# Two transfers over 128 partitions cut into pieces of 32 partitions, in a fused attention and two-layer MLP kernel

## The chip, the cores and the metric

The kernel runs on one core of one Trainium2 chip. The metric is the device time in microseconds (us), the median of several executions. One further execution was taken with the hardware profiler, and its trace is what the prediction reads.

## The reference

Three stages are fused. The input arrays q, k and v have the shape (1, 6016, 256).

```
qn = q / (norm(q, axis=1) + 1e-6);  kn = k / (norm(k, axis=1) + 1e-6)
s = kn.T @ qn / tau                     # 256 x 256, summed over the 6016 rows
a = softmax(s, axis=-1)
x = v @ a                               # 6016 x 256
x = elu(x @ moe_w_in) @ moe_w_out       # 256 -> 2048 -> 256
x = silu(x @ moe2_w_in) @ moe2_w_out    # 256 -> 2048 -> 256
```

## The kernel before

The 6016 rows are 47 blocks of 128, in six groups of eight blocks (the last has seven). The program has three parts.

**Start.** The arrays q and k stream through a buffer named `ring`; TensorE sums the scores, ScalarE and VectorE the squares of the columns (`sums`). Towards its end the first group of v is loaded into the tile `v0` by two transfers (line 461), each of 512 KB: 128 partitions by 4 blocks of 256 numbers. The row `i*32 + b*8 + j` of the group goes to partition `32*b + i`, and the view of v on the DRAM side therefore has `b` (4) outermost and `i` (32) inside it. After the softmax TensorE transposes `v0` (line 491).

**Main part.** From line 520 on the operations are recorded, put in an order by `in_order` with costs that the kernel states, and then emitted. All recorded operations go through a few helpers, so that one line stands for many of them: line 229 is every matrix product, line 200 every ScalarE operation, line 206 every VectorE operation on two tensors, and line 218 every transfer. Layer 1 runs over the six groups, then layer 2. Weights come through the buffers `st`, are converted (`cv`), and end in `wa`, `a21` and `wo`; the later groups of v come through `big`, eight transfers of 32 partitions for a group, in runs of 128 bytes. The tile `wa` lies in the memory of `v0`, so its first writers wait for the transfers into `v0` too.

**End.** The last group is stored by `y_store_final`, once for each half (`half` is 1, then 0): VectorE copies one PSUM bank (line 799) and ScalarE another into a `big` buffer, and one transfer of 512 KB stores it. The DRAM side of it is `rows_of[:, :, ...]`, with `b` outermost again.

Every transfer is issued by SyncE (SP), in the program's order. Eight completion semaphores, which the rows of the program's order name DMAHW0 to DMAHW7, are used in rotation: a transfer takes the next one, and SP first waits until the transfer eight before it, which used the same one, has landed.

Of the kernel before, what the change touches and what calls it, by code (L numbers as in the profile page):

```python
# [19 lines left out]
P = 128  # L20
# [19 lines left out]
V = namedtuple("V", "ap keys")  # L40
# [67 lines left out]
def channel_attention_elu_silu(  # L108
# [28 lines left out]
    nc = tc.nc  # L137
# [6 lines left out]
    TJ = 4  # L144
# [9 lines left out]
    vv = v.rearrange("b n c -> (b n) c")  # L154
# [9 lines left out]
    v0 = one.tile([P, GJ, C], F32, tag="wa", name="v0")  # L164
# [12 lines left out]
    def do(engine, n, emit, reads, writes, times=1):  # L177
        fixed, each, late, own = COST[engine]
        o = Op(
            engine,  # L180
            times * (fixed + each * n),
            late,
            own,
            emit,
            [k for v in reads if isinstance(v, V) for k in v.keys],
            [k for v in writes for k in v.keys],
        )
        if recording:
            ops.append(o)
        else:  # L190
            emit()
# [10 lines left out]
    def copy(out, src, **kw):  # L202
        act(out, src, AF.Copy, **kw)
# [13 lines left out]
    def dma(out, src):  # L217
        do("SP", 0, lambda: nc.sync.dma_start(out.ap, src.ap), [src], [out])  # L218
# [28 lines left out]
    def part(v, ap, *what):  # L247
        return V(ap, tuple(v.keys[0]._replace(what=x) for x in what))
# [15 lines left out]
    def y_bank(i):  # L264
        return V(y_ps[i], (("y", i),))
# [99 lines left out]
    with tc.manual_schedule():  # L365
# [92 lines left out]
        j0, nj0 = groups[0]  # L458
        for n in range(2):
            s = slice(n * nj0 // 2, (n + 1) * nj0 // 2)  # L460
            nc.sync.dma_start(v0[:, s], vv[: nj0 * P].rearrange("(i b j) c -> b i j c", i=32, b=4)[:, :, s])
        x, nr, r, t1, hx = nsq[:, 0:4], small[:, 4:8], small[:, 8:12], small[:, 12:16], small[:, 28:32]
        nc.scalar.activation(nr, x, AF.Sqrt)
        nc.scalar.activation(small[:, 25:26], one_sb, AF.Exp)
# [328 lines left out]
        def y_store_final(half):  # L793
            j0, nj = groups[order[final][1]]
            o = bigs.take()
            n = TJ * C
            y = [y_bank(2 * half + i) for i in range(2)]
            o0, o1 = (part(o, o.ap[:, i * n // 2 : (i + 1) * n // 2], i) for i in range(2))
            do("DVE", n // 2, lambda: nc.vector.tensor_copy(o0.ap, y[0].ap), [y[0]], [o0])
            copy(o1, y[1])  # L800
            rows_of = out[j0 * P : (j0 + nj) * P].rearrange("(i b j) c -> b i j c", i=32, b=4)
            dma(
                V(rows_of[:, :, half * TJ : (half + 1) * TJ], ()),
                part(o, o.ap[:, :n].rearrange("p (j c) -> p j c", j=TJ), 0, 1),
            )


        m_group(0)
# [4 lines left out]
        for s in range(len(steps) + 1):  # L813
            prev = s - 1
            now = s < len(steps)
            if now:
                n, j = steps[s]
# [17 lines left out]
            if s:  # L835
                second(prev, (0, 1))
                if steps[prev] == (final, NP - 1):
                    y_store_final(1)
                second(prev, (0, 0))
                if steps[prev][1] == NP - 1:  # L840
                    if steps[prev][0] == final:
                        y_store_final(0)
                    else:
                        y_store(steps[prev][0])
# [36 lines left out]
```

## Time and profile before

| what | value |
| --- | --- |
| median of 3 executions | 1088.67 us (1086.88 to 1089.07) |
| the profiled execution | 1089.08 us |
| its span, first to last instruction | 1087.3 us |
| TensorE busy | 1051.7 us, 97% |
| VectorE busy | 850.9 us, 78% |
| ScalarE busy | 718.0 us, 66% |
| mean granted TensorE clock | 0.987 |

The profiled execution lies 0.41 us above the median, and 1.78 us of it lie outside the span. Times in the rows below count from the start of the span. A busy share is an average over the span; what a change at one place is worth is read at that place.

### The profile page before, as it was taken

What the parts mean: (1) busy time and instruction counts of PE and PEld (TensorE: products, weight loads), DVE (VectorE), ACT (ScalarE), POOL (GpSimd) and SP (SyncE); (2) the same over time, 40 slices, a digit from 0 to 9 for tenths busy, and PEclk for the clock granted to TensorE, in tenths of its full rate; (3) what the DMA queues carried; (4) which work ended last, traced back from release to release, by engine and by line L of the source; (5) the groups of instructions that cost most, each with busy time, mean ns of one, the idle gap of its engine ahead of it and who ended that gap; (6) DMA issues with size and microseconds to landing.
All of it is one profiled execution on the core that took longest, in us unless ns stands there. A gap on an engine that the chain in (4) does not pass through costs nothing.

```text
span 1087.3 us, 13435 instructions
## 1 busy us (share of the span) xinstructions
PE 1051.7 (97%) x4878; PEld 889.5 (82%) x4878; DVE 850.9 (78%) x1433; ACT 718.0 (66%) x1305; POOL 0.8 (0%) x7
## 2 busy tenths in 40 slices
PE   9879999999999999999999999999999999999994
PEld 8757887887887888888898888998888888888994
DVE  4889999879979979979989975668668668667551
ACT  4578997777777768768779854555555555555541
POOL 0000000000000000000000000000000000000000
PEclk9988999999999999999999999999999999999997
DMA  9742225003003002001102402003003003002001
GB/s 344 210 93 78 83 87 141 1 1 77 1 1 68 11 1 55 18 1 57 41 1 89 154 1 68 11 1 74 1 1 78 1 1 78 1 1 39 1 1 39
DMA packets 99938, 54.60 MB, mean 50 GB/s; under 512 B 82848, under 2 KB 84640, under 8 KB 99232
## 3 DMA queue, kind: packets, MB, share of 16 engines
q1 hardware_dynamic: 99872, 53.75, 17.7%
q8 instruction: 38, 0.62, 0.2%
q14 instruction: 28, 0.23, 0.1%
HBM read 41.42 MB, written 12.32 MB: 49 GB/s over the span
## 4 chain that ended last, share of the span: by engine, by line
PE 83%; DVE 5%; ACT 4%; DMA 3%; SPq 2%; issue 1%; DVEq 0%
PE y L229 44%; PE h L229 39%; ACT e L200 2%; SPq L218 2%; DVE sums L443 1%; DVE h L206 1%; DMA st<-in_moe_w_in_dram 1%; ACT gs L200 1%; DMA big<-in_v_dram 1%; DVE gs L206 1%; DVE e L212 1%; DMA ring<-in_k_dram 1%; DVE e L763 1%; ACT xs L200 0%; DMA big<-yd 0%
## 5 line engine op out<-in xcount | busy, mean ns | idle before, releaser
L229 PE MATMUL y<-gs,wo 128*128 128x512 f32 (+1 forms) x2112 | 504.1, 387 | 11.0 <-ACT wo L200 6.8
L229 PE MATMUL h<-xs,wa 128*128 128x512 f32 (+1 forms) x1968 | 472.7, 385 | 1.8 <-DVE e L212 1.5
L229 PEld LDWEIGHTS y<-gs,wo 128*128 128x128 f32 x2112 | 396.8, 188 | 89.6 <-DVE e L763 8.0
L229 PEld LDWEIGHTS h<-xs,wa 128*128 128x128 f32 x1968 | 368.4, 188 | 71.1 <-DVE e L212 1.9
L206 DVE TENSOR_TENSOR h<-h,h 128x512 f32<-128x512 f32 (+1 forms) x400 | 269.5, 674 | 86.9 <-PE h L229 78.0
L206 DVE TENSOR_TENSOR gs<-e,gs 128x512 fp32r<-128x512 f32 (+1 forms) x384 | 257.8, 675 | 69.3 <-ACT e L200 65.3
L200 ACT ACTIVATE e<-h 128x512 f32<-128x512 f32 (+1 forms) x384 | 230.4, 601 | 80.8 <-DVE h L206 71.5
L200 ACT ACTIVATE gs<-h 128x512 fp32r<-128x512 f32 (+1 forms) x192 | 117.1, 610 | 151.2 <-DVE h L206 100.5
L212 DVE SCALAR_TENSOR_TENSOR e<-e,h 128x512 f32<-128x512 f32 (+1 forms) x192 | 128.4, 673 | 28.3 <-ACT e L200 28.1
L200 ACT ACTIVATE gs<-e 128x512 fp32r<-128x512 f32 (+1 forms) x192 | 117.0, 614 | 14.9 <-DVE e L212 14.9
L200 ACT ACTIVATE e<-e 128x512 f32<-128x512 f32 (+1 forms) x192 | 117.8, 618 | 2.8
L200 ACT ACTIVATE h<-h 128x512 f32<-128x512 f32 (+1 forms) x80 | 46.3, 579 | 39.2 <-PE h L229 39.0
L206 DVE TENSOR_TENSOR xs<-big,xs 128x512 fp32r<-128x512 f32 (+1 forms) x74 | 48.4, 671 | 5.0 <-ACT xs L200 5.0
L200 ACT ACTIVATE xs<-big 128x512 fp32r<-128x512 f32 (+1 forms) x74 | 43.3, 615 | 11.5 <-DMA big<-yd 8.8
L229 PEld LDWEIGHTS y<-wo,gs 128*128 128x128 f32 x384 | 47.9, 192 | 1.1
L229 PE MATMUL y<-wo,gs 128*128 128x256 f32 x384 | 48.3, 283 | 0.0
L391 PE MATMUL y<-ring 128*128 128x256 f32 x188 | 42.9, 390 | 0.5 <-DMA ring<-in_k_dram 0.5
L391 PEld LDWEIGHTS y<-ring 128*128 128x128 f32 x188 | 36.7, 197 | 5.9 <-issue 0.8
L443 DVE TENSOR_TENSOR sums<-sums 128x2048 f32<-128x2048 f32 (+2 forms) x16 | 27.1, 1691 | 13.6 <-ACT sums L441 13.0
L441 ACT ACTIVATE sums<-ring 128x2048 f32<-128x2048 f32 (+2 forms) x17 | 23.4, 1379 | 13.3 <-DMA ring<-in_k_dram 7.2
L200 ACT ACTIVATE cv<-st 128x512 f32<-128x512 f32 x32 | 21.4, 671 | 11.0 <-DMA st<-in_moe_w_in_dram 8.7
L229 PE MATMUL h<-xs,a 128*128 128x512 f32 x96 | 27.4, 392 | 0.5 <-DVE a L206 0.5
(91 smaller groups left out, 352.4 us busy)
## 6 DMA issues: line engine op xcount, KB each, us to landing
st<-in_moe_w_in_dram SPq DMA_DIRECT2D x16, 512.0 KB, 5.1
st<-in_moe_w_out_dram SPq DMA_DIRECT2D x16, 512.0 KB, 3.5
yd<-e SPq DMA_DIRECT2D x20, 256.0 KB, 2.4
big<-yd SPq DMA_DIRECT2D x5, 1024.0 KB, 4.7
ring<-in_q_dram SPq DMA_DIRECT2D x9, 512.0 KB, 7.3
ring<-in_k_dram SPq DMA_DIRECT2D x9, 512.0 KB, 7.3
big<-in_v_dram SPq DMA_DIRECT2D x32, 128.0 KB, 3.1
out_dram<-big SPq DMA_DIRECT2D x32, 128.0 KB, 3.4
```

Of the source, the lines that this page charges most:

```text
L200: do("ACT", width(out.ap), lambda: nc.scalar.activation(out.ap, src.ap, func, **kw), [src], [out])
L206: do("DVE", width(out.ap), lambda: nc.vector.tensor_tensor(out.ap, a.ap, b.ap, op), [a, b], [out])
L212: do("DVE", width(out.ap), lambda: nc.vector.scalar_tensor_tensor(out.ap, a.ap, s, b.ap, op0, op1), [a, b], [out])
L218: do("SP", 0, lambda: nc.sync.dma_start(out.ap, src.ap), [src], [out])
L229: nc.tensor.matmul(out.ap, lhs[a].ap, rhs[b].ap, start=start and a + b == 0, stop=stop and a == 1, **kw)
L391: nc.tensor.matmul(o_c[m][:, :C], ring[:, 1, j % RJ, m * P : (m + 1) * P], ring[:, 0, j % RJ], start=j == 0, stop=j == NJ - 1,)
L441: nc.scalar.activation(dst[:, :, :nj], ring[:, :, j0 % RJ : j0 % RJ + nj], AF.Square)
L443: nc.vector.tensor_tensor(acc[:, :, :nj], acc[:, :, :nj], dst[:, :, :nj], ALU.add)
L763: do("DVE", m, lambda t=t, y=y: nc.vector.tensor_copy(t.ap, y.ap), [y], [t])
```

## The change

The two loads of `v0` become eight, and the two stores of the last group become eight. For each `b` there is a transfer of 32 partitions and 128 KB, and the view on the DRAM side has `i` (32) outermost. The same bytes go between the same places.

```diff
@@ the load of v0
         for n in range(2):
             s = slice(n * nj0 // 2, (n + 1) * nj0 // 2)
-            nc.sync.dma_start(v0[:, s], vv[: nj0 * P].rearrange("(i b j) c -> b i j c", i=32, b=4)[:, :, s])
+            for b in range(4):
+                rows_of = vv[: nj0 * P].rearrange("(i b j) c -> b i j c", i=32, b=4)[b]
+                nc.sync.dma_start(v0[32 * b : 32 * (b + 1), s], rows_of[:, s])
@@ y_store_final
             rows_of = out[j0 * P : (j0 + nj) * P].rearrange("(i b j) c -> b i j c", i=32, b=4)
-            dma(
-                V(rows_of[:, :, half * TJ : (half + 1) * TJ], ()),
-                part(o, o.ap[:, :n].rearrange("p (j c) -> p j c", j=TJ), 0, 1),
-            )
+            for b in range(4):
+                dma(
+                    V(rows_of[b, :, half * TJ : (half + 1) * TJ], ()),
+                    part(o, o.ap[32 * b : 32 * (b + 1), :n].rearrange("p (j c) -> p j c", j=TJ), 0, 1),
+                )
```

On SP, at the end of the program, the last rows of its queue read as follows before (the sizes are those of the destination, `4x32x1024` is `b`, `i` and the 1024 numbers of a run; the names in brackets are the semaphores waited for).

```order
L218 DMA out_dram<-big_84 4x32x1024 [waits DMAHW3_49,DVE_49,Activation_49]
L218 DMA out_dram<-big_85 4x32x1024 [waits DMAHW4_49,DVE_49,Activation_49]
```

And now:

```order
L218 DMA out_dram<-big_84 32x1024 [waits DMAHW1_49,DVE_49,Activation_49]
L218 DMA out_dram<-big_84 32x1024 [waits DMAHW2_49]
L218 DMA out_dram<-big_84 32x1024 [waits DMAHW3_49]
L218 DMA out_dram<-big_84 32x1024 [waits DMAHW4_49]
L218 DMA out_dram<-big_85 32x1024 [waits DMAHW5_49,DVE_49,Activation_49]
L218 DMA out_dram<-big_85 32x1024 [waits DMAHW6_49]
L218 DMA out_dram<-big_85 32x1024 [waits DMAHW7_49]
L218 DMA out_dram<-big_85 32x1024 [waits DMAHW0_49]
```

The eight stores use each semaphore once, so that none of them waits for another of the eight; the first of each half waits for the two copies, as before.

On SP, at the load of `v0`, in one piece of the difference (`st` are weights, `v_66` is the tile `v0`):

```order
-L461 DMA v_66<-in_v_dram 128x1x1024 [waits DMAHW5_49]
-L461 DMA v_66<-in_v_dram 128x1x1024 [waits DMAHW6_49]
-L218 DMA st_86<-in_moe_w_in_dram 128x2x512 [waits DMAHW7_49,DVE_49]
-L218 DMA st_87<-in_moe_w_in_dram 128x2x512 [waits DMAHW0_49,DVE_49]
+L463 DMA v_66<-in_v_dram 32x1024 [waits DMAHW5_49]
+L463 DMA v_66<-in_v_dram 32x1024 [waits DMAHW6_49]
+L463 DMA v_66<-in_v_dram 32x1024 [waits DMAHW7_49]
+L463 DMA v_66<-in_v_dram 32x1024 [waits DMAHW0_49]
+L463 DMA v_66<-in_v_dram 32x1024 [waits DMAHW1_49]
+L463 DMA v_66<-in_v_dram 32x1024 [waits DMAHW2_49]
+L463 DMA v_66<-in_v_dram 32x1024 [waits DMAHW3_49]
+L463 DMA v_66<-in_v_dram 32x1024 [waits DMAHW4_49]
```

The two loads of weights, and the eight loads of `big` after them, stand behind eight issues now instead of two, and the first two of them wait for the landing of pieces of `v0`.

On TensorE the transposes of `v0` are the only rows that wait for more than before; the order of its instructions, like that of VectorE and ScalarE, is the same.

```order
-L491 MATMUL y_72<-ident,v_66 128x128 [waits DMAHW5_49]
+L493 MATMUL y_72<-ident,v_66 128x128 [waits DMAHW6_49,DMAHW7_49,DMAHW5_49,DMAHW0_49]
-L491 MATMUL h_76<-ident,v_66 128x128 [waits DMAHW6_49]
+L493 MATMUL h_76<-ident,v_66 128x128 [waits DMAHW3_49,DMAHW4_49,DMAHW2_49,DMAHW1_49]
```

Each of the two groups of transposes waits for four pieces instead of one transfer; the first writers of `wa` on ScalarE and VectorE wait for eight instead of two.

## Rows read from the trace of the kernel before

**Rows 1.** The page: span, engines' busy time, chain that ended last by engine.

```profile
span 1087.3 us, 13435 instructions
PE 1051.7 (97%) x4878; PEld 889.5 (82%) x4878; DVE 850.9 (78%) x1433; ACT 718.0 (66%) x1305; POOL 0.8 (0%) x7
...
PE 83%; DVE 5%; ACT 4%; DMA 3%; SPq 2%; issue 1%; DVEq 0%
```

**Rows 2.** ScalarE in order of time, 1069 to 1073 us: start, duration, instruction, idle before.

```profile
1071.75 0.60 ACT L200 ACTIVATE big<-y 128x512 f32<-128x512 f32 x1 [0.84 <-PE y L229]
```

**Rows 3.** SP's own queue in order of time, 1070 to 1088 us.

```profile
1070.93 0.61 SPq L218 DMA_DIRECT2D out_dram<-big  x1
...
1072.37 0.57 SPq L218 DMA_DIRECT2D out_dram<-big  x1
```

**Rows 4.** SP's waits, 1070 to 1088 us: sum, times, longest.

```profile
SPq L876 <- DMA out_dram<-big: 13.3, 2, 8.4
```

**Rows 5.** The end by stretches: stretch, us, busy, clock, share of 16 engines, GB/s.

```profile
1070.00:1072.00 2.00, 1.71 (x15) 1.51 (x13) 0.97 (x2) 0.85 (x2) 0.00 (x0) 1.00 0.00 0
1072.00:1074.00 2.00, 0.00 (x0) 0.00 (x0) 0.00 (x0) 0.34 (x1) 0.00 (x0) 1.00 0.24 47
1074.00:1076.00 2.00, 0.00 (x0) 0.00 (x0) 0.00 (x0) 0.00 (x0) 0.00 (x0) 0.94 0.24 43
1080.00:1082.00 2.00, 0.00 (x0) 0.00 (x0) 0.00 (x0) 0.00 (x0) 0.00 (x0) 0.50 0.26 106
1085.00:1086.00 1.00, 0.00 (x0) 0.00 (x0) 0.00 (x0) 0.00 (x0) 0.00 (x0) 0.50 0.11 45
1086.00:1087.30 1.30, 0.00 (x0) 0.00 (x0) 0.00 (x0) 0.00 (x0) 0.00 (x0) 0.50 0.00 0
```

**Rows 6.** SP's queue, 990 to 1003 us: the stores of the group before.

```profile
993.04 5.99 SPq L218 DMA_DIRECT2D out_dram<-big  x8
```

**Rows 7.** Two stretches while they moved; columns as in rows 5.

```profile
994.00:996.00 2.00, 2.00 (x16) 1.88 (x15) 1.90 (x4) 0.00 (x0) 0.00 (x0) 1.00 0.91 155
996.00:998.00 2.00, 2.00 (x17) 1.91 (x17) 0.78 (x2) 1.16 (x2) 0.00 (x0) 1.00 1.04 176
```

**Rows 8.** The first loads of q, 128 KB each (issue durations), and their landing.

```profile
L384 SPq DMA_DIRECT2D ring<-in_q_dram x3: 389/431/434, 0.7 to 2.6; - x3
...
DMA to landing us min/median/max: 2.1/2.2/2.7
```

**Rows 9.** Those eight stores of 32 partitions, 128 KB each: issue to landing.

```profile
DMA to landing us min/median/max: 3.2/3.5/3.6
```

**Rows 10.** The same part by stretches; columns as in rows 5.

```profile
52.00:54.00 2.00, 2.00 (x11) 2.00 (x11) 0.00 (x0) 0.00 (x0) 0.00 (x0) 0.50 0.28 109
66.00:68.00 2.00, 1.50 (x7) 0.69 (x6) 2.00 (x6) 1.74 (x5) 0.00 (x0) 1.00 0.06 10
85.00:89.30 4.30, 4.27 (x10) 3.40 (x11) 4.30 (x10) 1.54 (x3) 0.00 (x0) 0.50 0.16 62
```

**Rows 11.** The two weight loads behind v0: issue to landing.

```profile
DMA to landing us min/median/max: 17.6/18.0/18.5
```

**Rows 12.** SP's queue around the load of v0, by window.

```profile
40.36 1.36 SPq L461 DMA_DIRECT2D v<-in_v_dram  x2
41.82 1.01 SPq L218 DMA_DIRECT2D st<-in_moe_w_in_dram  x2
...
42.88 21.46 SPq L218 DMA_DIRECT2D big<-in_v_dram  x8
```

**Rows 13.** TensorE in order of time, 58 to 64 us.

```profile
58.57 0.61 PE L478 MATMUL h<-e,ones 128*128 128x256 f32 x2
59.02 1.04 PE L491 MATMUL y<-ident,v 128*128 128x128 f32 x8
59.89 1.04 PE L491 MATMUL h<-ident,v 128*128 128x128 f32 x8
...
62.49 0.44 PE L509 MATMUL h<-ident,e 128*128 128x128 f32 x2 [0.45 <-ACT e L504]
```

**Rows 14.** First readers: of the weights (ScalarE), of big (VectorE).

```profile
L200 ACT ACTIVATE cv<-st x2: 657/660/664, 68.3 to 68.9; 128x512 f32<-128x512 f32 x2
...
L215 DVE STREAM_TRANSPOSE big<-big x2: 1241/1242/1242, 78.6 to 89.2; 128x1024 f32<-128x1024 f32 x2
```

**Rows 15.** VectorE at 64.8 us, a wait for eight semaphores of transfers.

```profile
64.79 0.69 DVE L206 TENSOR_TENSOR xs<-h,xs 128x512 fp32r<-128x512 f32 x1 [0.24 <-DMA big<-in_v_dram]
```

## The prediction, made before the changed kernel ran

> **What bounds the kernel now.** The page first [rows 1]: TensorE is busy 97% of the span and stands for 83% of the chain that ended last. A change that only touches transfers can therefore pay only where TensorE is not the bound, and I look at the two places it touches. The end comes first. The last arithmetic is ScalarE's copy into `big`, from 1071.75 to 1072.35 us [rows 2]; SP issues the two stores at 1070.93 and 1072.37 us [rows 3]; and the span runs to 1087.3 us. That leaves about 15 us in which no engine computes. SP's waits say what they are: after its last issue SP waits 13.3 us in two waits for `out_dram<-big` [rows 4]. The second issue ends at 1072.94, so the last store lands at about 1072.94 + 13.3 + 0.1 = 1086.3, and 1.0 us of closing work follows it. The share of the transfer engines says why the stores are so slow [rows 5]: it is 0.24 to 0.26 while both move, four engines of sixteen, and the four move only 43 to 47 GB/s at first and 106 GB/s later. The two stores are 1.05 MB; at 106 GB/s alone they need 9.9 us. Four is also the count of `b`, the outermost dimension of the old view.
>
> **The end: cost of the pieces.** Do pieces of 32 partitions use more engines? The nearest rows are the stores of the group before, eight transfers of 128 KB from 32 partitions each, with 32 outermost: while they move, the share is 0.91 to 1.04 [rows 6, 7]. So I take all sixteen. They move runs of 128 bytes, ours runs of 4 KB, so their 155 to 176 GB/s is a floor for the rate. At that floor a piece of 131 KB takes at most 0.8 us; with sixteen engines at the 26 GB/s that each of four reaches at 106 GB/s, it takes 0.3 us. The pieces are then paced by SP's issues.
>
> What an issue costs: 0.43 us for the loads of q at the start, which are also 128 KB (128 runs) [rows 8], and 5.99 / 8 = 0.75 us for the stores of 1024 runs [rows 6]. Ours have 32 runs, so they lie nearer to the first; with 0.04 us between issues I take 0.47. From issue to landing it takes 2.1 to 2.2 us for those loads on an idle queue [rows 8], and 3.2 to 3.6 us for the stores of small runs [rows 9]; again I take the nearer one, 2.2, and keep 3.5 as the bound.
>
> The sum: the first piece goes out at 1070.93, as the first store does now. Four issues of 0.47 last to 1072.81, by which time ScalarE's second copy (1072.35) is done, so that the second four follow without a gap. The last is issued at 1070.93 + 7 × 0.47 = 1074.2 and lands at 1076.4. Against 1086.3 that is 9.9 us less; the 1.0 us behind it stays. Bounds: issues of 0.38 and 2.1 us give 1075.7, 10.6 us less; issues of 0.75 and 3.5 us give 1079.7, 6.6 us less. I take no term for the slow first microseconds of the old stores (43 to 47 GB/s against 106); if they slow the first four pieces likewise, up to 1 us of the gain goes, which the upper bound holds.
>
> [...]
>
> **The load of v0.** Here I look for who waits. In the stretch 52 to 54 us the share is 0.28 and the rate 109 GB/s, four engines again [rows 10]. The transfers stand in the way of those behind them: the two weight loads take 17.6 to 18.5 us to land [rows 11], and SP needs 21.46 us to issue the eight loads of `big` [rows 12]. It looks bad, yet nobody pays for it. TensorE goes from the product at 58.57 through both groups of transposes (59.02, 59.89) without idle time, so `v0` has landed by then [rows 13]. The weights are issued between 41.82 and 42.83 [rows 12] and land by 42.8 + 18.5 = 61.3; ScalarE reads them first at 68.3 [rows 14]. The loads of `big` have landed when the share falls to 0.06, by 68; VectorE transposes them from 78.6 on [rows 10, 14]. So the weights have a cover of 7 us and `big` of 10 us; how much `v0` itself has, no row says, only that it is enough.
>
> With the change SP issues eight pieces, 8 × 0.47 = 3.8 us instead of 1.36, and everything behind them leaves 2.4 us later; but on sixteen engines 1.05 MB is gone in 3 to 6 us (at 416 and at 176 GB/s) instead of at least 9.9, so all three land earlier. They feed nothing that waits, so I put the gain at nothing. The cover is what hides it; if `v0` were late, each microsecond would go straight into the softmax chain of the start.
>
> **The added waits.** The first transposes, and the first writers of `wa` on ScalarE and VectorE, wait for more semaphores. The nearest row is a wait of VectorE for eight of them at 64.79 us, with 0.24 us idle before it [rows 15]; the trace puts it down to a load of `big`, which that instruction doesn't read, so I take it as the price of the waits themselves. Queued behind the transposes are fillers and the transposes of the softmax, before the second of which TensorE idles 0.45 us for ScalarE anyway [rows 13]: no cost on TensorE up to that. On VectorE and ScalarE it costs between 0 and 0.24 us each; I take 0, which is within the rounding of the 9.9.
>
> **Sum.** Of the profiled execution's 1089.08 us, 9.9 go: 1079.2. That execution lies 0.41 above the median, so a median should come to 1078.8. I forecast 1079.0.
>
> **Rivals.**
> [...]
> 2. *The pieces stay on four engines*, since each draws on a quarter of the partitions. Then 1.05 MB takes 9.9 us at the later rate, or 14 at today's mix: landing at 1082 to 1086, a time of 1085 to 1088.7, at worst no change. Against it stands the share of 0.91 to 1.04 for pieces of 32 partitions [rows 7].
> 3. *Slower: the pieces follow one another.* If each store had to land before the next moved, eight of 2.2 us last 17.6 us from 1070.93 and end at 1088.5, 2.2 us later than now: 1090.9. It decides from (1086.3 - 1070.93 - 2.2) / 7 = 1.9 us between pieces. Against it: the earlier eight were issued in 5.99 us, 0.75 apart, though each took 3.5 us to land [rows 6, 9], so several were under way at once. [...]
> 4. *The start moves.* TensorE's granted clock is 0.50 in 85 to 89.3 us, where it is busy 4.27 us [rows 10]. If small shifts remove or add such a stretch, the time moves by about 2.1 us either way, on top of the 9.9.
>
> **Chances.** All sixteen engines, paced by issues: 0.65. Half the ports: 0.20. Four engines: 0.05. One after another: 0.03. The start moves by about 2 us: 0.07. The range goes from 1077.0 (the lower bound of the issues with a start 1 us better) to 1081.6 (issues and landings near the dear end, or half the ports with a worse start); outside it lie rivals 2 and 3 and the rest of the dear end. A difference within 0.2%, 2.2 us, can't be told from none, since the runs before already span that much. Faster: 0.94; same: 0.03 (most of the dear side of rival 2); slower: 0.03 (rival 3).
>
> **What the changed profile would show.** At the end: eight stores from 1070.9 to about 1074.6, about 0.47 us apart; a share near 0.5 to 1.0 for some 4 us instead of 0.25 for 14; SP's closing wait about 2 us instead of 13.3; a span near 1077.4. [...] At the start: weight loads that land in less than 10 us, not 18; issues of `big` within 7 us, not 21; and TensorE at the softmax and ScalarE at `cv` at the same times as now. The prediction is wrong if pieces are issued more than 0.75 us apart, if the share at the end stays at 0.25, or if the product at 58.57 or the first layer begins more than a microsecond away from where it does now.

## The result, and the profile after

The changed kernel takes 1078.58 us (median of 6 executions, 1076.64 to 1080.33), the kernel before 1088.17 us in the same set (6 executions). The ratio is 0.9914, with a 95% interval of 0.990 to 0.9927: faster by 9.6 us. The forecast was 1079.0 us, in a range of 1077.0 to 1081.6.

The page of the profiled execution (1078.04 us), the rows that answer to [rows 1]:

```profile
span 1076.3 us, 13457 instructions
PE 1050.3 (98%) x4878; PEld 888.7 (83%) x4878; DVE 850.9 (79%) x1433; ACT 718.1 (67%) x1305; POOL 0.8 (0%) x7
...
PE 86%; DVE 6%; ACT 3%; DMA 2%; issue 1%; SPq 1%; DVEq 0%
```

The busy times of the engines are those of before within 1.4 us. What has gone is time in which no engine works. ScalarE in order of time, at the end of the changed kernel:

```profile
1070.60 0.60 ACT L200 ACTIVATE big<-y 128x512 f32<-128x512 f32 x1 [0.84 <-PE y L229]
```

SP's queue there, the eight stores as one row (start of the first, time to the end of the last):

```profile
1069.79 3.62 SPq L218 DMA_DIRECT2D out_dram<-big  x8
```

The transfers into the output in that stretch: how long an issue takes in ns, and how long it is from issue to landing:

```profile
L218 SPq DMA_DIRECT2D out_dram<-big x8: 352/422/427, 1069.8 to 1073.0; - x8
...
DMA to landing us min/median/max: 2.0/2.3/2.5
```

SP's wait behind them:

```profile
SPq L879 <- DMA out_dram<-big: 1.7, 1, 1.7
```

And the stretches, with columns as in [rows 5]: the last three are the granted clock, the share of sixteen transfer engines, and GB/s.

```profile
1071.00:1072.00 1.00, 0.00 (x0) 0.00 (x0) 0.00 (x0) 0.20 (x1) 0.00 (x0) 1.00 0.82 209
1072.00:1073.00 1.00, 0.00 (x0) 0.00 (x0) 0.00 (x0) 0.00 (x0) 0.00 (x0) 1.00 0.91 270
1073.00:1074.00 1.00, 0.00 (x0) 0.00 (x0) 0.00 (x0) 0.00 (x0) 0.00 (x0) 1.00 0.96 287
1074.00:1075.00 1.00, 0.00 (x0) 0.00 (x0) 0.00 (x0) 0.00 (x0) 0.00 (x0) 0.66 0.65 172
1075.00:1076.00 1.00, 0.00 (x0) 0.00 (x0) 0.00 (x0) 0.00 (x0) 0.00 (x0) 0.50 0.00 0
```

In the first three of these stretches the share is 0.82 to 0.96 where it was 0.24 to 0.26 [rows 5], and the stores last about 4 us instead of 14. SP's closing wait falls from 13.3 us [rows 4] to 1.7.

A measure that is used for every kernel below: the **tail**, from the end of ScalarE's last copy to the end of the span. Before it is 1087.3 - 1072.35 = 14.95 us, after it 1076.3 - 1071.20 = 5.10 us, so 9.85 us went there. The span of the profiled execution is 11.0 us shorter, since the copy itself ends 1.15 us earlier; the first experiment asks whether that belongs to the change.

At the start, SP's queue in the changed kernel:

```profile
39.59 3.78 SPq L463 DMA_DIRECT2D v<-in_v_dram  x8
43.47 0.91 SPq L218 DMA_DIRECT2D st<-in_moe_w_in_dram  x2
44.42 11.77 SPq L218 DMA_DIRECT2D big<-in_v_dram  x8
```

The landing of the two weight loads:

```profile
DMA to landing us min/median/max: 6.5/6.9/7.4
```

TensorE around the transposes of `v0`:

```profile
57.97 0.60 PE L480 MATMUL h<-e,ones 128*128 128x256 f32 x2
58.41 1.04 PE L493 MATMUL y<-ident,v 128*128 128x128 f32 x8
59.28 1.04 PE L493 MATMUL h<-ident,v 128*128 128x128 f32 x8
...
61.88 0.44 PE L511 MATMUL h<-ident,e 128*128 128x128 f32 x2 [0.45 <-ACT e L506]
```

The weights land after 7 us instead of 18 [rows 11], the loads of `big` are issued in 11.8 us instead of 21.5 [rows 12], and TensorE passes the transposes without idle time, as before [rows 13], with the same 0.45 us before the softmax's second transposes.

### The profile page after: what moved, and what is told of

Same layout as the page of the kernel before. It is cut to its first block, busy times and chain, and to the rows that moved or that the text cites. A ratio compares the mean times of both kernels' runs of the same rounds, so it can differ in the third digit from the quotient of the medians.

```text
span 1076.3 us, 13457 instructions
## 1 busy us (share of the span) xinstructions
PE 1050.3 (98%) x4878; PEld 888.7 (83%) x4878; DVE 850.9 (79%) x1433; ACT 718.1 (67%) x1305; POOL 0.8 (0%) x7
## 4 chain that ended last, share of the span: by engine, by line
PE 86%; DVE 6%; ACT 3%; DMA 2%; issue 1%; SPq 1%; DVEq 0%
PE y L229 45%; PE h L229 40%; ACT e L200 2%; DVE sums L443 2%; DVE h L206 1%; DMA st<-in_moe_w_in_dram 1%; ACT gs L200 1%; DMA ring<-in_k_dram 1%; DVE gs L206 1%; DVE e L765 1%; PE y L391 1%; DVE e L212 1%; DMA big<-in_v_dram 0%; ACT xs L200 0%; DVE xs L206 0%
## 5 line engine op out<-in xcount | busy, mean ns | idle before, releaser
L443 DVE TENSOR_TENSOR sums<-sums 128x2048 f32<-128x2048 f32 (+2 forms) x16 | 27.0, 1691 | 13.3 <-ACT sums L441 12.7
```

Of the source, the lines that this page charges most:

```text
L443: nc.vector.tensor_tensor(acc[:, :, :nj], acc[:, :, :nj], dst[:, :, :nj], ALU.add)
```

## The experiments

A ratio is to the kernel before, run on the same chip; the tail is from the profile.

| kernel | ratio, 95% interval | median us | tail us |
| --- | --- | --- | --- |
| before | | 1088.17 | 14.95 |
| changed | 0.9914 (0.990 to 0.9927) | 1078.58 | 5.10 |
| load alone | 1.000 (0.9987 to 1.0013) | 1089.23 | 15.04 |
| stores alone | 0.9905 (0.9884 to 0.9926) | 1079.05 | 5.22 |
| stores of 64 partitions | 1.0071 (1.0052 to 1.0091) | 1096.66 | 23.74 |
| stores of 16 partitions | 0.9939 (0.9916 to 0.9961) | 1082.68 | 8.43 |
| changed, again | 0.9912 (0.9897 to 0.9927) | 1078.87 | 5.03 |
| two queues | 0.9928 (0.9912 to 0.9944) | 1080.81 | 5.17 |
| two queues, other pairs | one execution | 1076.01 | 4.71 |
| load of 64 partitions | 0.9969 (0.9956 to 0.9983) | 1085.15 | 5.18 |
| other rows, one store a half | 0.9904 (0.9887 to 0.9921) | 1077.32 | 3.71 |
| other rows, four stores a half | 0.9919 (0.9903 to 0.9935) | 1079.18 | 4.98 |

### One part alone

The first kernel keeps the old stores, the second the old load of `v0`.

```diff
 load alone, y_store_final as before:
-            for b in range(4):
-                dma(V(rows_of[b, :, ...], ()), part(o, o.ap[32 * b : 32 * (b + 1), :n]...))
+            dma(V(rows_of[:, :, ...], ()), part(o, o.ap[:, :n]...))
 stores alone, v0 as before:
-            for b in range(4):
-                nc.sync.dma_start(v0[32 * b : 32 * (b + 1), s], ...)
+            nc.sync.dma_start(v0[:, s], ...)
```

> Only the load of v0 is cut into eight pieces; the stores at the end are the two old ones. My theory: nobody waits for v0, the weights behind it or big, so the time is that of before within 0.2% (ratio 0.998 to 1.002), although the two weight loads land in under 10 us instead of 18 and SP issues the eight loads of big in some 11 us instead of 21. SP's closing wait stays near 13 us. Rival: the changed kernel's last copy on ScalarE ended at 1071.20 instead of 1072.35 us; if the cut load earned that, this kernel is 0.6 to 1.2 us faster (ratio 0.9989 to 0.9994) and its last copy ends near 1071.2 in the trace.

> Only the two stores at the end are cut into eight pieces; v0 is loaded by the two old transfers. My theory: the whole gain is here, 9.8 us (ratio 0.991), with the weight loads still landing after 17 to 18 us and SP's closing wait near 2 us. Rival: 1.1 us of the gain come from the load, so that this kernel gains 8.7 us (ratio 0.992).

The load alone gives 1.000, and its last copy ends at 1072.66 us, no earlier than before. The stores alone give 0.9905 and a tail of 5.22 us. So the gain is the stores', and the load earns nothing that can be measured. The rival's 0.6 to 1.2 us would still lie inside the interval of the load alone, which excludes only more than 1.4 us; against it stands that last copy. In the kernel with the load alone the weights do land earlier, after 6.5 to 8.1 us:

```profile
DMA to landing us min/median/max: 6.5/7.3/8.1
```

This is a transfer two and a half times as fast that changes nothing, because its first reader comes at 68.3 us [rows 14] and was served by 61.3 already. The 1.15 us by which the changed kernel's last copy ended earlier are within the scatter: the same kernel, profiled again, ends it at 1070.47, and two kernels further down that are the same program up to their last stores end it at 1069.49 and at 1074.33.

### What sets the number of engines

```diff
-            for b in range(4):
+            for b in range(0, 4, 2):
                 dma(
-                    V(rows_of[b, :, half * TJ : (half + 1) * TJ], ()),
-                    part(o, o.ap[32 * b : 32 * (b + 1), :n]...),
+                    V(rows_of[b : b + 2, :, half * TJ : (half + 1) * TJ], ()),
+                    part(o, o.ap[32 * b : 32 * (b + 2), :n]...),
                 )
```

> As the changed kernel, but each half of the last output is stored by two transfers of 64 partitions and 256 KB, with b (now 2) outermost, four in all. My theory: the number of transfer engines is the count of the outermost dimension, so each piece runs on two engines, and on the same two: a share of 0.13, some 52 GB/s at best, 1.05 MB in 20 us or more. The end then takes 6 to 9 us longer than in the kernel before and 16 to 19 us longer than in the changed one (ratio to before 1.005 to 1.009). Rival: what helps is that more and smaller transfers are under way at once; then four pieces lie between two and eight, about 5 us faster than before (ratio 0.995).

Four stores of 64 partitions are slower than two of 128: ratio 1.0071, a tail of 23.74 us, 8.8 more than before. A stretch of that end:

```profile
1078.00:1082.00 4.00, 0.00 (x0) 0.00 (x0) 0.00 (x0) 0.00 (x0) 0.00 (x0) 0.50 0.13 52
```

A share of 0.13 is two engines, at 26 GB/s each. With 4 outermost the share was 0.26, with 2 it is 0.13, with 32 it reaches 0.96; more and smaller transfers alone do not help. So the count of engines that the shares give is that of the outermost dimension with 2 and with 4; with 32 it is at most 0.96 x 16 = 15.4.

### Twice as many pieces

```diff
             for b in range(4):
-                dma(...)
+                for u in range(2):
+                    dma(
+                        V(rows_of[b, 16 * u : 16 * (u + 1), half * TJ : (half + 1) * TJ], ()),
+                        part(o, o.ap[32 * b + 16 * u : 32 * b + 16 * (u + 1), :n]...),
+                    )
```

> As the changed kernel, but with the stores cut once more: sixteen pieces of 16 partitions and 64 KB, 16 outermost. My theory: sixteen engines, paced by SP's issues of 0.46 us: the last is issued 15 x 0.46 = 6.9 us after the first instead of 3.2, and lands 2 us later, so the time is 3.5 us above the changed kernel and 6.3 below the kernel before (ratio 0.994). [...]

The ratio is 0.9939, as forecast by the issues, and the tail 3.3 us longer than the changed kernel's. SP's queue and the landing of the sixteen:

```profile
1067.86 7.29 SPq L218 DMA_DIRECT2D out_dram<-big  x16
```

```profile
DMA to landing us min/median/max: 1.9/2.0/2.0
```

7.29 / 16 = 0.46 us for a store, and every one lands 1.9 to 2.0 us after its issue: nothing queues, and the issues pace this kernel. But a stretch shows something else:

```profile
1071.00:1073.00 2.00, 0.00 (x0) 0.00 (x0) 0.00 (x0) 0.00 (x0) 0.00 (x0) 0.87 0.80 148
```

148 GB/s at a share of 0.80 are 148 / 12.8 = 11.6 GB/s for each busy engine, where four engines reached 25.5 (106 at 0.26, [rows 5]). Engines are busy longer with the same 4 KB.

### Issues taken off SP

```diff
             for b in range(4):
-                dma(...)
+                dst = V(rows_of[b, ...], ())
+                src = part(o, o.ap[32 * b : 32 * (b + 1), :n]...)
+                if b in ((2, 3), (3,))[half]:
+                    do("ACT", 0, lambda d=dst, s=src: nc.scalar.dma_start(d.ap, s.ap), [src], [dst])
+                else:
+                    dma(dst, src)
```

The entry at 1 is the first half that is stored, as `half` is 1, then 0. The second kernel has `((1, 3), (3,))` there.

> The changed kernel once more, beside the next one: 0.991 of the kernel before.

> As the changed kernel, but three of the eight stores are issued by ScalarE: b = 3 of the first half, b = 2 and 3 of the second. My theory: SP's issues, 0.46 us each, pace the stores. SP has issued its three of the first half by 1071.2, when the second copy ends, and two issues on each queue follow, the last at 1071.7 instead of 1072.98: about 1.2 us less than the changed kernel (ratio to before 0.990 where that has 0.991), and the last landing 2.8 us behind the end of the last copy instead of 4.1. [...]

> As the kernel with two queues, but in the second half ScalarE has b = 1 and 3 and SP b = 0 and 2, so that the pieces under way together are b = 0 with 1 and 2 with 3, where before they were 0 with 2 and 1 with 3. [...]

The changed kernel repeats its 0.991. With two queues nothing is gained: 0.9928, and a tail of 5.17 us where 3.8 was expected. ScalarE's part of the end, with two queues:

```profile
1073.73 0.60 ACT L200 ACTIVATE big<-y 128x512 f32<-128x512 f32 x1 [0.84 <-DVE big L801]
1074.36 0.85 ACTq L808 DMA_DIRECT2D out_dram<-big  x2
```

The last issues, SP's included, begin 0.4 us after the copy's end, where the changed kernel's begins 1.8 us after it. The landing takes the time back:

```profile
DMA to landing us min/median/max: 2.1/3.4/3.8
```

So my theory that SP's issues alone pace the eight stores falls: with the issues 1.4 us earlier, the last landing does not come earlier. Pieces of 32 partitions are paced by the moving of their data as well, and the rate of the full stretches stays at 238 to 295 GB/s:

```profile
1073.00:1074.00 1.00, 0.70 (x6) 0.49 (x5) 0.69 (x1) 0.27 (x1) 0.00 (x0) 1.00 0.31 66
1074.00:1075.00 1.00, 0.00 (x0) 0.00 (x0) 0.00 (x0) 0.33 (x1) 0.00 (x0) 1.00 0.93 295
1075.00:1076.00 1.00, 0.00 (x0) 0.00 (x0) 0.00 (x0) 0.00 (x0) 0.00 (x0) 1.00 0.90 238
1076.00:1077.00 1.00, 0.00 (x0) 0.00 (x0) 0.00 (x0) 0.00 (x0) 0.00 (x0) 1.00 0.89 287
```

The first of these stretches moves 66 / (0.31 x 16) = 13 GB/s for a busy engine, the later ones 17 to 20. The other pairing has 246 at 0.77 and 311 at 0.95, 20 each, and a tail shorter by 0.5 us, in the one execution that it has. Whether it matters which pieces are under way together stays open.

The mean rates also hide something. Two short stretches of the changed kernel, with one queue:

```profile
1071.30:1071.80 0.50, 0.00 (x0) 0.00 (x0) 0.00 (x0) 0.00 (x0) 0.00 (x0) 1.00 1.01 221
1071.90:1072.20 0.30, 0.00 (x0) 0.00 (x0) 0.00 (x0) 0.00 (x0) 0.00 (x0) 1.00 1.01 396
```

At the same share the rate is 13.7 GB/s for each engine in the first and 24.5 in the second, with pieces of the same size, 32 partitions each and from the same queue. So pieces of 32 partitions move at two speeds, and 16 to 20 is a mean over both. What decides between them no run shows.

The two kernels with two queues are the same program up to their last stores, yet their profiled spans differ by 5.3 us. That comes from the start. The stretch 50 to 62 us, first of one, then of the other; TensorE's granted clock is the third figure from the end:

```profile
50.00:62.00 12.00, 9.77 (x46) 9.25 (x47) 4.94 (x19) 3.19 (x6) 0.00 (x0) 0.57 0.63 104
```

```profile
50.00:62.00 12.00, 10.94 (x69) 9.63 (x70) 5.54 (x24) 4.93 (x13) 0.00 (x0) 0.86 0.47 73
```

TensorE's first transposes of `v0` in order of time, in the same two kernels:

```profile
60.74 1.04 PE L493 MATMUL y<-ident,v 128*128 128x128 f32 x8
```

```profile
56.56 1.04 PE L493 MATMUL y<-ident,v 128*128 128x128 f32 x8
```

The first transposes lie 4.2 us apart. TensorE's first instructions after an idle time come before them, at 52.23 us in the first kernel and at 50.37 us in the second:

```profile
52.23 3.58 PE L423 MATMUL h<-ones,sums 128*128 128x1 f32 x16 [4.00 <-DVE sums L443]
```

```profile
50.37 2.01 PE L423 MATMUL h<-ones,sums 128*128 128x1 f32 x16 [3.57 <-DVE sums L443]
```

So 1.9 us of the 4.2 stand already there. The other 2.3 us come between these instructions and the transposes, where the granted clock is lower in the first kernel: a mean of 0.57 from 50 to 62 us, as the stretches above show, against 0.86 in the second. This is why tails, and not spans, are compared here.

### What the cover of v0 is worth

```diff
-            for b in range(4):
-                rows_of = vv[: nj0 * P].rearrange("(i b j) c -> b i j c", i=32, b=4)[b]
-                nc.sync.dma_start(v0[32 * b : 32 * (b + 1), s], rows_of[:, s])
+            for b in range(0, 4, 2):
+                rows_of = vv[: nj0 * P].rearrange("(i b j) c -> b i j c", i=32, b=4)[b : b + 2]
+                nc.sync.dma_start(v0[32 * b : 32 * (b + 2), s], rows_of[:, :, s])
```

> As the changed kernel, but each half of v0 is loaded by two transfers of 64 partitions with b (2) outermost. My theory: they run on two engines, 1.05 MB at 52 GB/s take 20 us from about 41.5, so v0 lands at 62 us or later where TensorE wants it at 58.4 and 59.3, and the softmax and the first layer start 3 to 7 us later: a time 3 to 7 us above the changed kernel (ratio to before 0.994 to 0.998). This is what v0's cover is worth: the old transfers were enough, half their rate isn't. Rival: TensorE's fillers and the wait for the softmax take it up, and the time stays that of the changed kernel (ratio 0.991).

TensorE at the second group of transposes:

```profile
65.50 1.97 PE L493 MATMUL h<-ident,v 128*128 128x128 f32 x8 [3.87 <-DMA v<-in_v_dram]
```

It waits 3.87 us for `v0`, and the median is 6.3 us above that of the changed kernel in the same set. Behind the wait the eight transposes take 1.97 us instead of 1.04; the rest of the 6.3 us is not traced. The load isn't free: two engines (a share of 0.13 and 48 GB/s from 44 to 50 us) are too slow for it, four were enough (0.28 and 109 GB/s, [rows 10]), and sixteen (0.98 and 250 GB/s in the changed kernel, 42 to 44 us) earn nothing more.

### Another order of rows, and a version with a shorter tail

The last group's transposes in layer 1 write its columns in another order, and partition p of the last output then holds rows 8p to 8p+7 of the group. The view on the DRAM side has 128 outermost, so one store for a half runs on sixteen engines (a share of 0.97 to 1.02, below). The second kernel keeps the new rows but cuts each store into four.

```diff
 x_made, for the group that is last in layer 2:
-    xf[:, c, : nj * P].rearrange("p (j b i) -> p b j i", j=nj, i=32)
+    xf[:, c, : nj * P].rearrange("p (j i b) -> p b j i", j=nj, i=32)
 y_store_final:
-            rows_of = out[j0 * P : (j0 + nj) * P].rearrange("(i b j) c -> b i j c", i=32, b=4)
-            for b in range(4):
-                dma(V(rows_of[b, :, ...], ()), part(o, o.ap[32 * b : 32 * (b + 1), :n]...))
+            rows_of = out[j0 * P : (j0 + nj) * P].rearrange("(p j) c -> p j c", p=P)
+            dma(V(rows_of[:, half * TJ : (half + 1) * TJ], ()), part(o, o.ap[:, :n]...))
```

> The last group's columns are written in the order (j, i, b) instead of (j, b, i) by its transposes in layer 1, so that partition p of the last output holds the rows 8p to 8p+7, and one transfer of 128 partitions, with 128 outermost on both sides, stores each half: two stores again, but on sixteen engines. [...] Rival: stores to this array have their own limit near 245 GB/s, whatever the partitions; then 0.52 MB take 2.1 us and the landing comes 3.7 us behind the copy. If only SP's issues counted, it would be 2.2 to 2.5.

> The same order of columns and rows, but each half stored by four pieces of 32 partitions again. Runs that follow each other in a piece now lie 8 KB apart in memory instead of 32 KB. [...] Rival: the 32 KB between the runs slowed the stores; then each busy engine moves 25 GB/s and the issues alone pace them, with the last landing about 3.7 us behind the copy.

Two stretches of the kernel with one store a half, and the landing of its two stores:

```profile
1070.60:1071.60 1.00, 0.00 (x0) 0.00 (x0) 0.00 (x0) 0.58 (x1) 0.00 (x0) 1.00 1.02 422
...
1072.00:1073.00 1.00, 0.00 (x0) 0.00 (x0) 0.00 (x0) 0.00 (x0) 0.00 (x0) 1.00 0.97 401
```

```profile
DMA to landing us min/median/max: 2.6/2.6/2.7
```

401 GB/s at a share of 0.97 are 25.8 GB/s for each busy engine, and the tail falls to 3.71 us, 1.4 less than the changed kernel's, 11.2 less than before. Stores to this array have no limit of their own near 245 GB/s. Cut into four pieces each, with runs 8 KB apart instead of 32 KB, the same rows give 4.98 us and the old rate:

```profile
1073.00:1074.00 1.00, 0.00 (x0) 0.00 (x0) 0.00 (x0) 0.00 (x0) 0.00 (x0) 1.00 0.91 266
```

That is 18 GB/s for each busy engine. So it isn't the distance between the runs. What is left between the two kernels is the number of partitions that a transfer covers, and its size with it (512 KB against 128 KB): in the mean 128 partitions give 25.8, 32 give 16 to 20, 16 give 11.6. No run changes one of the two alone. Size by itself does not explain the pieces of 32 partitions, which move at two speeds with one size. Why fewer partitions go with a lower rate in the mean, no run shows.

This version has the shortest tail of all. Its time, 1077.32 us, ratio 0.9904, isn't shown to be less than the changed kernel's 0.9912: the intervals overlap. The 1.4 us show in the tail alone, since the scatter of the start is larger.

## Why the prediction was right, and where it wasn't

- **Where the time is.** Right. The wait behind the last stores was 13.3 us of SP's time with no engine at work; 9.85 us of the tail went, against 9.9 forecast, and with the load alone nothing measurable was gained.
- **Sixteen engines instead of four.** Right, and shown from both sides: 2 outermost give a share of 0.13 and a slower kernel, 4 give 0.26, 32 give up to 0.96. Rival 2 is refuted by these shares, rival 3 by stores issued 0.46 us apart that land 2.0 to 2.5 us later.
- **0.47 us for an issue, 2.2 us to the landing.** Measured 3.62 / 8 = 0.45 and 2.0 to 2.5. The choice of the nearer row (few runs) held; the dear end, 0.75, belongs to stores of 1024 runs.
- **What paces the pieces.** Wrong in part: the step "the pieces are then paced by SP's issues" doesn't stand alone. In the changed kernel the sum came out term by term, seven steps of 0.46 and 2.3 us to the landing. But with issues 1.4 us earlier the tail stays at 5.17 us. The data of eight pieces, 1.05 MB at some 240 GB/s, take about 4.4 us, and eight issues take 3.6 plus the last piece's landing; the two limits lie so close together here that the sum came out right, which is in part luck. The pieces do not get 26 GB/s for each engine in the mean: the full stretches had 209 to 287 GB/s at shares of 0.82 to 0.96, 16 to 19 for each. Half the ports, which the chances and the range name, is a term that no run shows; what the runs showed in its place is pieces at two speeds, 13.7 and 24.5 GB/s for each engine, which landed 2.0 to 2.5 us after their issue in the changed kernel and up to 3.8 with two queues.
- **The load of `v0`: nothing gained.** Right: 1.000. That it must not be slower is shown by 3.87 us of waiting on two engines. The issues of `big` took 11.8 us where I had written within 7. One of the eight alone lasted 4.7 us, and what held it no run shows:

```profile
L218 SPq DMA_DIRECT2D big<-in_v_dram x8: 663/698/4668, 44.4 to 55.5; - x8
```

  It costs nothing, since `big` is read at 78 us.
- **The added waits.** No idle time before either group of transposes, and VectorE's wait for eight semaphores has 0.24 us before it again, as in [rows 15]. The trace now names ScalarE for it, which speaks against the load of `big` as the cause before; no run separates it from the price of the waits.
- **Rival 4, a start that moves.** It moves from one profiled execution to the next: the same kernel's last copy ended at 1071.20 and at 1070.47 us, and with other last stores between 1069.3 and 1074.3. With the load alone the copy ended 0.31 us later than before, so no part of the change in it shows, but it sets how well one execution can be read. The product at 58.57 us began at 57.97 in the changed kernel, within the microsecond that the prediction allowed.

## What to carry to other kernels

Read the share of the transfer engines in a stretch as a count: 0.25 is four engines, 0.13 two, and the outermost dimension of the DRAM view is the first thing to look at when it stays at such a value. Cutting the transfer along that dimension repairs that at a price of 0.46 us of issue for each piece and, in the mean, at a lower rate for each engine (16 to 20 GB/s, where the four had 25.5); a layout that lets one transfer over all 128 partitions do it gave a shorter tail (3.7 us instead of 5.1). A transfer behind which nobody waits earns nothing by being faster (the load alone: a ratio of 1.000), so the first question is which wait ends last there.

## What was not expected

- Transfer engines that are busy aren't equally productive: 25.8, 16 to 20 and 11.6 GB/s for each in the mean, with 128, 32 and 16 partitions in a transfer and the same 4 KB runs. Loads differ likewise: the loads of q and k at the start of the kernel before and the pieces of `v0` in the changed one stand against each other in these rows, first the old kernel, then the new one.

```profile
10.00:20.00 10.00, 9.54 (x45) 8.22 (x44) 4.58 (x2) 5.47 (x5) 0.00 (x0) 1.00 1.03 408
```

```profile
42.00:44.00 2.00, 2.00 (x11) 1.77 (x10) 1.90 (x2) 1.06 (x1) 0.00 (x0) 1.00 0.98 250
```

  That is 408 / 16.5 = 25 GB/s for each busy engine with 128 partitions, and 250 / 15.7 = 16 with 32. But 128 partitions alone don't give the high rate: the first loads of q and k, of 128 and 256 KB in shorter runs, move 16 and 13 GB/s for each busy engine in two stretches of the kernel before.

```profile
3.00:4.00 1.00, 1.00 (x6) 1.00 (x6) 0.03 (x1) 0.61 (x1) 0.00 (x0) 1.00 0.85 220
4.00:5.00 1.00, 1.00 (x7) 1.00 (x6) 0.69 (x1) 0.09 (x2) 0.00 (x0) 1.00 0.91 195
```
- The old stores ran at half rate for their first microseconds, 47 GB/s at a share of 0.24, and then at 106 GB/s at 0.26 [rows 5]. Why is open; no run tested it.
- Two queues issue earlier but land later: 3.4 us from issue to landing in the median, where one queue has 2.3.
